# Conversions of the dense weights at other steps of the attention, a second buffer for their squares, and one choice of clusters that ends later

## Chip, cores and metric

One Trainium2 chip, one of its NeuronCores. The metric is the time of one execution on the device in microseconds, lower is better. TensorE (PE) multiplies, VectorE (DVE), ScalarE (ACT) and GpSimd (POOL) work on tiles, SyncE (SP) issues most transfers.

## The reference

The program is a chain of three layers. `q`, `k`, `v` have the shape (2, 8, 768, 64), with 16 clusters for each head.

```python
def _attn_ref(q, k, v, centroids):
    ...
    q_assign = np.argmax(np.einsum('bhsd,hcd->bhsc', q_n, c_n), axis=-1)
    k_assign = np.argmax(np.einsum('bhsd,hcd->bhsc', k_n, c_n), axis=-1)
    mask = q_assign[:, :, :, None] == k_assign[:, :, None, :]
    scores = scale * np.matmul(q, k.transpose(0, 1, 3, 2))
    scores = np.where(mask, scores, -1000000000.0)
    ...
    return np.matmul(attn, v).astype(np.float32)      # softmax over the allowed keys

def reference(**kwargs):
    attn_out = _attn_ref(**attn_kwargs)
    x = attn_out.transpose(0, 2, 1, 3).reshape(B * S, H * D)          # 1536 x 512
    x = _moe_ref(x=x, **moe_kwargs)    # each token to the best of 8 experts: relu(x @ w1[e]) @ w2[e], gated
    return _moe2_ref(x=x, **moe2_kwargs)   # h = x @ w_in; (h * sigmoid(1.702 h)) @ w_out, 2048 wide
```

The weights `w_in` and `w_out` of the last layer arrive as 64-bit floats.

## The kernel before

The kernel runs three stages one after another: attention (to about 265 us of the span), the experts, the dense layer. The change touches the attention alone.

**Units and steps.** Attention has 8 units u, each two heads of one batch entry. A unit has 12 steps, a step is one head and 128 queries against all 768 keys; there are 96 steps, and step i belongs to unit i // 12. The remainder r = i % 12 says where in its unit a step is. One turn i of the loop issues, in this order: the scores `sp` of step i + 1 (four matmuls on PE, L496 and L497) and their maximum `nm` (DVE, L499), pieces of the next units' preparation, conversions of dense weights, products with v, the transposes `pt` of step i - 1 (PE, L513) with their copies `pT` (first half on ACT, L518, second half on DVE, L520), and the exponential `P` of step i + 1 (ACT, L505). Each engine works through its own list in this order, so one instruction that waits holds up all behind it on that engine. The n-th `nm` in the trace is therefore a clock of the steps.

**Long and short steps.** In two places of a unit, at r = 2, 3 and at r = 8, 9, PE also multiplies with v: `po`, 24 matmuls (L548). Their result goes through `oa` on ACT (L554) and `pox` on PE (L567) to `xw` on DVE (L569).

**Preparation of a unit.** A table PLAN says at which step each of the ten pieces of a later unit is issued: transposes of q and k (`pqk`, PE, with `Fq`, `Fk` on ACT and `Hq`, `Lq`, `Hk`, `Lk` on POOL) and stacks (DMAs on SP to `Q`, `X`, `Z`), cluster scores (`pcl`, PE), and on DVE the choice of a cluster: `by_token` and `argmax_a` (L408 and L378 to L380), `argmax_b` (L387, a maximum `m2`), `chosen` (L392), `by_cluster` (L412); then `rows_of_ones` (ACT L416, 8 small DMAs `ohT` on SP). Piece 5 is issued late in r = 2, piece 6 (`argmax_b`) at the start of r = 3.

**Conversion of dense weights.** A quarter of the 64-bit weights (8 groups of 128 x 512 numbers out of 32) is turned into 32-bit numbers during the attention, and waits in DRAM (`wd`) for the dense layer. A group is loaded to `raw` (512 KB, SP), and four operations follow, named here after the code: `bits` (a square of the high word on ACT, L117, into the buffer `csq`, and a shift on DVE, L118), `top` (L121), `tail` (L124), `guard` (L127, which reads and overwrites `csq`). Behind `guard` stand a store of `csq` to `wd`, issued by POOL (L163), and the load of the next group. There is one `csq` buffer, so the square of the next group has to wait until that store has landed.

**What sets the order.** The dict `slots` says how many operations of this list step i issues:

```python
    slots = {12 * u + r: n for u in range(1, 5) for r, n in ((3, 1), (8, 1), (9, 2))}
    slots.update({11: 2, 68: 1, 69: 1, 75: 1, 80: 2, 81: 2, 86: 2, 87: 2, 92: 1, 93: 2})
    ...
            if i in (8, 11):
                load_early()
            for _ in range(slots.get(i, 0)):
                convert_early()
```

**Zeros.** `zrow` is 128 x 512 zeros; eight DMAs of 768 KB (`zero_rows`, L286) write them to `xd` at steps 14, 18, ... 42. Nobody reads `zrow` after that. From step 61 on, pieces of the routing of the first batch entry (`route(0)`) run between the attention's own operations, mostly on DVE and POOL.

Of the kernel before, what the change touches and what calls it, by code (L numbers as in the profile page):

```python
# [9 lines left out]
F32 = mybir.dt.float32  # L10
# [13 lines left out]
E = 8  # L24
# [21 lines left out]
def attention_moe_ffn(ctx: ExitStack, tc: tile.TileContext, q, k, v, centroids, w_gate, w_og, w1, w2, w_in, w_out, out):  # L46
# [3 lines left out]
    def f32(ap):  # L50
        return ap.bitcast(F32)
# [47 lines left out]
    def wide_load(pool, c, g):  # L99
        src = pair_of(w_in, w_out, c)[g // 2].bitcast(I32)  # L100
        t = pool.tile([128, 1024], I32, name="raw", tag="raw")
        if g < 2:
            nc.sync.dma_start(out=t.rearrange("p (k n) -> p k n", k=2), in_=src[:, 2 * g:2 * g + 2])
        else:
            nc.sync.dma_start(out=t, in_=src[:, g - 2])
        return t

    def wide_ops(pool, t, csq=2):

        r = t.rearrange("p (n w) -> p n w", w=2)  # L110
        l, h = r[:, :, 0], r[:, :, 1]
        hold = {}

        def bits():
            hold["t"] = pool.tile([128, 512], I32, name="ct", tag="ct", bufs=1)
            hold["s"] = pool.tile([128, 512], F32, name="csq", tag="csq", bufs=csq)
            nc.scalar.activation(hold["s"], f32(h), AF.Square)  # L117
            nc.vector.tensor_scalar(hold["t"], h, 3, 0x3FFFFFFF, op0=ALU.logical_shift_left, op1=ALU.bitwise_and)  # L118

        def top():  # L120
            nc.vector.scalar_tensor_tensor(hold["t"], h, -0x40000000, hold["t"], op0=ALU.bitwise_and, op1=ALU.bitwise_or)  # L121

        def tail():
            nc.vector.scalar_tensor_tensor(hold["t"], l, 29, hold["t"], op0=ALU.logical_shift_right, op1=ALU.bitwise_or)  # L124

        def guard():
            nc.vector.scalar_tensor_tensor(hold["s"], hold["s"], F64_TINY, f32(hold["t"]), op0=ALU.is_ge, op1=ALU.mult)  # L127
        return hold, [bits, top, tail, guard]
# [14 lines left out]
    cva = at.enter_context(tc.tile_pool(name="cva", reuse_waits="tile", bufs=2))  # L143
# [2 lines left out]
    ready = deque()  # L146
    convert = deque()

    def load_early():
        if early:  # L150
            c, g = early.pop(0)
            ready.append((c, g, wide_load(cva, c, g)))

    def convert_early():
        if not convert:
            if not ready:
                return
            c, g, t = ready.popleft()
            hold, ops = wide_ops(cva, t, 1)

            def last(f=ops[3]):
                f()
                nc.gpsimd.dma_start(out=wd[2 * c + g // 2][:, (g % 2) * 512:(g % 2) * 512 + 512], in_=hold["s"])  # L163
                load_early()
            convert.extend(ops[:3] + [last])
        convert.popleft()()
# [14 lines left out]
    fill = []  # L181
    scatters = []
    zrow = one.tile([128, DM], F32, name="zrow")

    def load_unit(u):
        b, pr = UNITS[u]
        d = st[u] = {}
        for nm, src in (("q", q), ("k", k), ("v", v)):
            t = ld.tile([128, 2, T, D], F32, name=f"ld_{nm}", tag=f"ld_{nm}", bufs=4 if nm == "v" else 2)
            nc.sync.dma_start(out=t, in_=src[b, 2 * pr:2 * pr + 2].rearrange("h (p t) d -> p h t d", t=T))  # L190
            d[nm] = t
# [16 lines left out]
    def setup_first():  # L208
        nc.vector.memset(idle, 0.0)
        keep_clock(7)  # L210
        nc.sync.dma_start(out=craw, in_=centroids.rearrange("h c d -> (h c) d"))
        load_unit(0)
        make_identity(nc, ident)
        nc.vector.tensor_copy(identb, ident)
        ii = one.tile([128, C], I32, name="ii")
        nc.gpsimd.iota(ii, [[-1, C]], base=C, channel_multiplier=0)
        nc.vector.tensor_copy(rev16, ii)
        nc.vector.memset(pen_scale[0:32], 1.0)
        nc.vector.memset(pen_scale[32:64], BIG)
        nc.vector.memset(pen_scale[64:80], BIG)  # L220
        nc.vector.memset(pen_bias[0:32], 0.0)
        nc.vector.memset(pen_bias[32:64], -BIG)
        nc.vector.memset(pen_bias[64:80], -BIG)

    def setup_centroids():
        nc.gpsimd.memset(nought, 0.0)

        csq = one.tile([128, D], F32, name="csq")
        cn = one.tile([128, 8], F32, name="cn")
        nc.vector.tensor_tensor(csq, craw, craw, op=ALU.mult)  # L230
        nc.vector.tensor_reduce(cn[:, 0:1], csq, op=ALU.add, axis=AX.X)
        nc.scalar.activation(cn[:, 1:2], cn[:, 0:1], AF.Sqrt)
        nc.scalar.activation(cn[:, 7:8], cn[:, 0:1], AF.Exp)
        nc.vector.tensor_scalar(cn[:, 2:3], cn[:, 1:2], 1e-30, None, op0=ALU.max)
        nc.vector.reciprocal(cn[:, 3:4], cn[:, 2:3])
        nc.vector.scalar_tensor_tensor(cn[:, 4:5], cn[:, 0:1], cn[:, 3:4], cn[:, 2:3], op0=ALU.mult, op1=ALU.add)
        nc.vector.tensor_scalar(cn[:, 5:6], cn[:, 4:5], 0.5, 1e-6, op0=ALU.mult, op1=ALU.add)
        nc.vector.reciprocal(cn[:, 6:7], cn[:, 5:6])
        cnorm = one.tile([128, 2, D], F32, name="cnorm")
        nc.vector.tensor_scalar(cnorm[:, 0], craw, cn[:, 6:7], None, op0=ALU.mult)  # L240
        nc.vector.tensor_copy(cnorm[:, 1], cnorm[:, 0])
        nc.vector.tensor_copy(cblk.rearrange("p h a c -> p (h a c)"), nought.to_broadcast([128, H * 4 * C]))
        return cnorm
# [236 lines left out]
    NS = len(steps)  # L480
# [279 lines left out]
            nc.vector.tensor_tensor(ci[:, b], t2, place[b], op=ALU.add)  # L760


    PLAN = ((0, 0, 0, 1, 3, 5, 6, 7, 8, 8), (-3, -2, 0, 1, 1, 2, 3, 8, 8, 9), (-2, -1, 0, 1, 1, 2, 3, 8, 8, 9))
    plan_at = {}
    for u in range(1, len(UNITS)):
        for n, r in enumerate(PLAN[min(u, 3) - 1]):
            plan_at.setdefault((12 * (u - 1) + r, n == 6, n == 5 and u > 1), []).append((u, n))
    pieces = {}

    def prepare(i, early=False, late=False):  # L770
# [3 lines left out]
            for f in pieces[u][n]:  # L774
                f()

    slots = {12 * u + r: n for u in range(1, 5) for r, n in ((3, 1), (8, 1), (9, 2))}
    slots.update({11: 2, 68: 1, 69: 1, 75: 1, 80: 2, 81: 2, 86: 2, 87: 2, 92: 1, 93: 2})

    with tc.manual_schedule():  # L780
        setup_first()
        first = prep_pieces(0)
        load_unit(1)
        cnorm = setup_centroids()
        for n, piece in enumerate(first):
            if n == 1:
                setup_blocks(cnorm)
            if n == 3:
                keep_clock(8)
            for f in piece:  # L790
                f()
        setup_rest()
        emit_scores(0)
        emit_exp(0)
        for i in range(NS + 2):
            nu, r = divmod(i + 3, 12)
            if i == 3 or r == 0 and nu + 2 < len(UNITS):
                load_unit(nu + 2)
            prepare(i, True)
            if i + 1 < NS:  # L800
                emit_scores(i + 1)
            tail = i >= NS - TAIL
            if (tail or i % 3 == 0) and ost:
                ost.popleft()()
            prepare(i)
            if i == 0:
                spots[:] = [(ps_m, "m")]
            if i >= 14 and i % 4 == 2 and len(fill) < E:
                zero_rows(len(fill))
            if i % (NS // 2) == NS // 2 - 4 and i < NS:  # L810
                sum_logits(i // (NS // 2))
            if i == NS // 2 + 13:
                routing.append(route(0))
            if i in (8, 11):
                load_early()
            for _ in range(slots.get(i, 0)):
                convert_early()
            for _ in range(2 if tail else 1):
                if av:
                    av.popleft()()  # L820
            prepare(i, False, True)
            if 0 <= i - 1 < NS:
                emit_pt(i - 1)
            n = i - (1 if tail else 2)
            if 0 <= n < NS and steps[n][2] % 3 == 2:
                queue_av(n)
            if i + 1 < NS:
                emit_exp(i + 1)
        advance(stop="weighed")
        while av:  # L830
            av.popleft()()
        while ost:
            ost.popleft()()
        advance()
        routing.append(route(2))
        advance()
        finish_routing()
        assert not (early or ready or convert)
        keep_clock_last(90)
# [315 lines left out]
    with tc.manual_schedule():  # L1155
# [23 lines left out]
        for g in range(G + 2):  # L1179
            e, c = divmod(g, 8)  # L1180
            nxt = wins.get(e + 1)
            r = c - (7 - nxt["nr"]) if nxt else 0
# [78 lines left out]
    with tc.manual_schedule():  # L1261
        gq = deque()
        for g in range(len(seq) + 2):
# [6 lines left out]
            if g >= 2:  # L1270

                for m in range(4) if g < len(seq) or g == len(seq) + 1 else ():
                    for g0, gh, gl in list(gq)[:1] if g < len(seq) else gq:
                        fh, tb, c, i = seq[g0]
# [47 lines left out]
```

## Time and profile before

| | |
|---|---|
| median of 3 runs | 744.75 us (744.46 to 746.16) |
| the profiled execution | 743.59 us, of which the span of its instructions 741.6 us |
| PE busy in the span | 709.2 us (96%) |
| DVE, ACT, POOL busy | 453.8, 390.2, 262.1 us |
| mean granted TensorE clock | 0.983 of full speed |

PE is called busy also while its pipelined matmuls are only being waited out, so 96% does not say that PE sets the time at each place. The rows below are from the same execution; their times count from the start of its span.

### The profile page before, as it was taken

The page shows a single profiled execution, that of the slowest core. Times are in us where ns is not written, and L with a number is a line of the kernel's source. Part 1 is how long each engine was busy: PE and PEld are TensorE (multiplying, and loading weights), DVE is VectorE, ACT ScalarE, POOL GpSimd, SP SyncE. Part 2 cuts the span into 40 slices and gives each one's busy share as a digit, 9 for nine tenths or more (in the row PEclk, how much of TensorE's full clock was granted, in tenths as well). Part 3 has the DMA queues.
Part 4 walks back from the last instruction along what each step waited for, and adds up shares of the span by engine and source line. Part 5 has one row for each costly group of instructions (what it writes and reads, how often), then busy time and mean ns, then how long its engine had stood idle before and what let it go on. Part 6 is the DMA issues. An engine that isn't in the chain of part 4 may idle for free.

```text
span 741.6 us, 12556 instructions
## 1 busy us (share of the span) xinstructions
PE 709.2 (96%) x4572; PEld 582.0 (78%) x4572; DVE 453.8 (61%) x855; ACT 390.2 (53%) x779; POOL 262.1 (35%) x216
## 2 busy tenths in 40 slices
PE   8999999999998887999999998999999999999996
PEld 5766786777766667999999897888888888888885
DVE  6969788789887772334554555687555656232322
ACT  7765675666755553455677776545434344222120
POOL 1230321303930033655778879122332212020202
PEclk9999999999999997999999999999999999999998
DMA  6779769555351037565576775134544211010101
GB/s 193 178 186 293 208 221 279 142 148 133 125 143 54 16 131 263 188 228 195 185 243 225 250 242 192 57 114 90 68 72 42 74 62 53 1 57 0 57 1 57
DMA packets 66689, 101.27 MB, mean 137 GB/s; under 512 B 9440, under 2 KB 44384, under 8 KB 66624
## 3 DMA queue, kind: packets, MB, share of 16 engines
q1 hardware_dynamic: 63680, 92.04, 43.4%
q0 software_dynamic: 2944, 8.40, 3.0%
q8 instruction: 37, 0.61, 0.4%
q14 instruction: 28, 0.23, 0.1%
HBM read 66.56 MB, written 14.69 MB: 110 GB/s over the span
## 4 chain that ended last, share of the span: by engine, by line
PE 59%; issue 18%; DVE 11%; ACT 6%; POOL 2%; DMA 2%; SPq 1%; POOLq 0%; ACTq 0%; DVEq 0%
PE pt L513 6%; PE po L548 6%; PE sp L496 4%; PE ph L1151 4%; PE ph L1150 4%; PE ph L1152 4%; PE sp L497 3%; PE py L1243 3%; PE py L1242 3%; PE py L1244 3%; ACT w L888 3%; PE py L974 2%; PE ph L974 2%; PE pox L567 2%; DVE nm L499 1%
## 5 line engine op out<-in xcount | busy, mean ns | idle before, releaser
L891 POOL TENSOR_TENSOR w<-raw,w 128x1024 fp32r<-128x1024 f32 x51 | 125.4, 2476 | 45.8 <-ACT w L888 30.5
L499 DVE TENSOR_REDUCE nm<-sp 128x1 f32<-128x768 f32 x96 | 91.6, 955 | 16.4 <-PE sp L497 14.5
L1227 DVE TENSOR_TENSOR sg<-ph,sg 128x512 f32<-128x512 f32 x48 | 33.2, 691 | 104.6 <-ACT sg L1226 104.2
L505 ACT ACTIVATE P<-sp,nm 128x768 f32<-128x768 f32 x96 | 87.5, 912 | 10.8 <-DVE nm L499 9.7
L513 PE MATMUL pt<-ident,P 128*128 128x128 f32 x576 | 84.4, 279 | 8.0 <-ACT pT L518 5.5
L513 PEld LDWEIGHTS pt<-ident,P 128*128 128x128 f32 x576 | 65.7, 142 | 32.5 <-issue 18.8
L1226 ACT ACTIVATE sg<-ph 128x512 f32<-128x512 f32 x48 | 28.7, 598 | 109.2 <-PE ph L1152 105.9
L1151 PE MATMUL ph<-ytl,w 128*128 128x512 f32 x192 | 76.1, 397 | 0.0
L1150 PE MATMUL ph<-yth,w 128*128 128x512 f32 x192 | 76.0, 396 | 0.0
L1152 PE MATMUL ph<-yth,w 128*128 128x512 f32 x192 | 75.5, 393 | 0.0
L924 POOL TENSOR_TENSOR w<-csq,w 128x512 fp32r<-128x512 f32 x24 | 32.8, 1365 | 120.5 <-ACT w L923 120.5
L1243 PE MATMUL py<-w,gh 128*128 128x512 f32 x192 | 75.3, 392 | 0.0
L496 PE MATMUL sp<-X,Q 128*128 128x384 f32 x192 | 74.0, 386 | 1.0 <-ACT P L505 0.9
L1242 PE MATMUL py<-w,gh 128*128 128x512 f32 x192 | 74.9, 390 | 0.0
L1244 PE MATMUL py<-w,gl 128*128 128x512 f32 x192 | 74.7, 389 | 0.0
L888 ACT CAST w<-raw 128x1024 fp32r<-128x1024 f32 x68 | 70.5, 1043 | 3.9 <-DMA raw<-in_moe_w_dram 3.9
L548 PE MATMUL po<-pT,ld_v 128*32 128x384 f32 x768 | 68.6, 490 | 0.0
L497 PE MATMUL sp<-Z,Q 80*128 80x384 f32 x192 | 65.9, 343 | 0.0
L518 ACT COPY pT<-pt 128x384 f32<-128x384 f32 x96 | 46.1, 480 | 37.5 <-PE pt L513 37.3
L974 PE MATMUL py<-ht,w 128*128 128x480 f32 (+5 forms) x192 | 60.8, 368 | 4.3 <-DVE ht L998 2.9
L520 DVE COPY pT<-pt 128x384 f32<-128x384 f32 x96 | 52.8, 550 | 14.1 <-PE pt L513 14.0
L974 PE MATMUL ph<-t,w 128*128 128x480 f32 (+5 forms) x192 | 60.3, 367 | 0.0
(253 smaller groups left out, 1504.9 us busy)
## 6 DMA issues: line engine op xcount, KB each, us to landing
raw<-in_moe_w_dram SPq DMA_DIRECT2D x64, 512.0 KB, 4.1
raw<-in_moe_w_in_dram SPq DMA_DIRECT2D x16, 512.0 KB, 5.2
raw<-in_moe_w_out_dram SPq DMA_DIRECT2D x16, 512.0 KB, 3.3
xd<-zrow SPq DMA_DIRECT2D x8, 768.0 KB, 6.5
Q<-Hq SPq DMA_DIRECT2D x28, 192.0 KB, 3.8
ld_q<-in_q_dram SPq DMA_DIRECT2D x8, 384.0 KB, 4.7
ld_k<-in_k_dram SPq DMA_DIRECT2D x8, 384.0 KB, 6.1
ld_v<-in_v_dram SPq DMA_DIRECT2D x8, 384.0 KB, 7.7
```

The lines of the kernel that those rows point to most:

```text
L496: nc.tensor.matmul(sp[:, n, :384], d["Q1"][:, h, cs], d["X"][:, h, ks], start=True, stop=False)
L499: nc.vector.tensor_reduce(nm, sp[:, :, :384], op=ALU.max, axis=AX.XY, negate=True)
L513: nc.tensor.transpose(pt[:, r * 128:(r + 1) * 128], L["P"][:, n, r * 128:(r + 1) * 128], ident)
L548: nc.tensor.matmul(po[32 * g:32 * g + 32, :384], v_[:, hh, tile_t(kt), 32 * a:32 * a + 32], pts[n][:, kt, :], start=kt < (2 if alone else ...
L891: (eng or nc.gpsimd).tensor_tensor(lo, r, f32(hi), op=ALU.subtract)
L974: nc.tensor.matmul(ps[:, :2 * n], w_hi, t, start=first, stop=False)
L1150: nc.tensor.matmul(ph, wa(key, 0, k, i), yth[:, k, cs], start=(k == 0), stop=False)
L1151: nc.tensor.matmul(ph, wa(key, 0, k, i), ytl[:, k, cs], start=False, stop=False)
L1152: nc.tensor.matmul(ph, wa(key, 1, k, i), yth[:, k, cs], start=False, stop=(k == 3))
L1242: nc.tensor.matmul(po[m], gh[:, ms], wb(key, 0, i), start=first, stop=False)
L1243: nc.tensor.matmul(po[m], gh[:, ms], wb(key, 1, i), start=False, stop=False)
L1244: nc.tensor.matmul(po[m], gl[:, ms], wb(key, 0, i), start=False, stop=last)
```

## The change

The same operations are done, on the same data. Four things move. (1) The first two loads of dense weights go from steps 8 and 11 to steps 15 and 18, and the table of conversions is shifted: nothing at 11, 15 and 20, three at 21, the pattern of r = 3, 8, 9 in units 2 to 5 instead of 1 to 4, and a new distribution from 75 on. (2) The square's buffer is one tile that is kept, and from step 48 on `zrow` is a second one; groups 3, 5 and 7 use it. (3) `argmax_b` of unit 2 goes from the start of step 15 to step 20, ahead of `chosen` and `by_cluster`. (4) With that, each operation lands in another kind of step, as this table shows (b = bits, t = top, l = tail, g = guard):

| step | 11 | 15 | 20 | 21 | 27 | 32 | 33 | ... | 63 | 68 | 69 | 75 | 80 | 81 | 86 | 87 | 92 | 93 |
|---|---|---|---|---|---|---|---|---|---|---|---|---|---|---|---|---|---|---|
| before | bt | l | g | bt | l | g | bt | | | l | g | b | tl | gb | tl | gb | t | lg |
| after | | | | btl | g | b | tl | | g | b | tl | g | b | tl | gbt | lg | bt | lg |

Steps 39, 44, 45 and 51, 56, 57 go as 27, 32, 33 do.

```diff
-    def wide_ops(pool, t, csq=2):
+    def wide_ops(pool, t, square=None):
...
-            hold["s"] = pool.tile([128, 512], F32, name="csq", tag="csq", bufs=csq)
+            hold["s"] = pool.tile([128, 512], F32, name="csq", tag="csq") if square is None else square
...
+    spare_squares = []
...
-            hold, ops = wide_ops(cva, t, 1)
+            if not spare_squares:
+                spare_squares.append(cva.tile([128, 512], F32, name="csq", tag="csq", bufs=1))
+            hold, ops = wide_ops(cva, t, spare_squares[(4 * c + g) % len(spare_squares)])
...
-    PLAN = ((0, 0, 0, 1, 3, 5, 6, 7, 8, 8), (-3, -2, 0, 1, 1, 2, 3, 8, 8, 9), (-2, -1, 0, 1, 1, 2, 3, 8, 8, 9))
+    PLAN = ((0, 0, 0, 1, 3, 5, 6, 7, 8, 8), (-3, -2, 0, 1, 1, 2, 8, 8, 8, 9), (-2, -1, 0, 1, 1, 2, 3, 8, 8, 9))
...
-            plan_at.setdefault((12 * (u - 1) + r, n == 6, n == 5 and u > 1), []).append((u, n))
+            plan_at.setdefault((12 * (u - 1) + r, n == 6 and u != 2, n == 5 and u > 1), []).append((u, n))
...
-    slots = {12 * u + r: n for u in range(1, 5) for r, n in ((3, 1), (8, 1), (9, 2))}
-    slots.update({11: 2, 68: 1, 69: 1, 75: 1, 80: 2, 81: 2, 86: 2, 87: 2, 92: 1, 93: 2})
+    slots = {12 * u + r: n for u in range(2, 6) for r, n in ((3, 1), (8, 1), (9, 2))}
+    slots.update({21: 3, 27: 1, 75: 1, 80: 1, 81: 2, 86: 3, 87: 2, 92: 2, 93: 2})
...
+            if i == NS // 2:
+                assert len(fill) == E
+                spare_squares.append(zrow)
-            if i in (8, 11):
+            if i in (15, 18):
                 load_early()
```

The list of PE is the same row for row. Three places on the other engines follow; line numbers behind the change are 4 to 7 higher.

ACT at steps 80 to 82 before: `P` is the exponential, `ohT` the one-hot rows of unit 7, the square into `csq` stands between `ohT` and `oa`.

```order
L518 COPY pT<-pt 128x3x128
L505 ACTIVATE P,sm<-sp,nm 128x768
L416 ACTIVATE ohT<-oT,oh_bias,oh_scale 128x384
L117 ACTIVATE csq<-raw 128x512
L554 COPY oa<-po 128x384
L518 COPY pT<-pt 128x3x128
```

ACT at the same steps of the change: the square stands one `pT` and one `P` earlier, and it writes `zrow`.

```order
L117 ACTIVATE zrow<-raw 128x512
L522 COPY pT<-pt 128x3x128
L509 ACTIVATE P,sm<-sp,nm 128x768
L420 ACTIVATE ohT<-oT,oh_bias,oh_scale 128x384
L558 COPY oa<-po 128x384
L522 COPY pT<-pt 128x3x128
```

So no square is left between `ohT` and `oa`; the same move was made at steps 33, 45 and 57, with `csq` or `zrow` as its buffer.

DVE at step 15 before, where unit 2's choice stands between the scores of unit 1:

```order
L380 TENSOR_TENSOR eq<-eq,rev_60 128x384
L520 COPY pT<-pt 128x3x128
L387 TENSOR_REDUCE m_911<-eq 128x24
L499 TENSOR_REDUCE nm<-sp 128x1
L569 TENSOR_TENSOR xw_107<-pox,rs 128x3x80
L124 SCALAR_TENSOR_TENSOR ct<-raw,ct 128x512
L520 COPY pT<-pt 128x3x128
L499 TENSOR_REDUCE nm<-sp 128x1
```

DVE at the same step of the change:

```order
L384 TENSOR_TENSOR eq<-eq,rev_60 128x384
L524 COPY pT<-pt 128x3x128
L503 TENSOR_REDUCE nm<-sp 128x1
L573 TENSOR_TENSOR xw_107<-pox,rs 128x3x80
L524 COPY pT<-pt 128x3x128
L503 TENSOR_REDUCE nm<-sp 128x1
```

The maximum L387 and the `tail` L124 are gone from here; the maximum stands at step 20 now, where `guard` stood.

SP behind the stacks of unit 2 in the change (`xd<-zrow` are the zero fills of steps 14 and 18, the first two loads of dense weights stand behind one each, then come the loads of unit 4 and the one-hot rows of unit 2):

```order
L290 DMA xd<-zrow 128x3x512
L103 DMA raw<-in_moe_w_in_dram 128x2x512
L290 DMA xd<-zrow 128x3x512
L103 DMA raw<-in_moe_w_in_dram 128x2x512
L194 DMA ld_q<-in_q_dram 128x2x384
L194 DMA ld_k<-in_k_dram 128x2x384
L194 DMA ld_v<-in_v_dram 128x2x384
L426 DMA Z<-ohT 16x384 x2
```

Before, both loads stood further up, one ahead of the loads of unit 3 and one ahead of the stacks of k, and the place here held two fills and the third load.

## Rows read from the trace of the kernel before

**Rows 1.** Timeline of ACT: squares at steps 11, 21 and 81, with their wait.

```profile
47.44 0.67 ACT L117 ACTIVATE csq<-raw 128x512 f32<-128x512 f32 x1 [3.68 <-DMA raw<-in_moe_w_in_dram]
...
74.06 0.66 ACT L117 ACTIVATE csq<-raw 128x512 f32<-128x512 f32 x1 [2.34 <-DVE rs L558]
...
227.20 0.66 ACT L117 ACTIVATE csq<-raw 128x512 f32<-128x512 f32 x1 [3.58 <-issue]
```

**Rows 2.** Timeline of PE: what it waited for behind two of them.

```profile
48.53 0.90 PE L567 MATMUL pox<-wl,oa 128*128 128x80 f32 x6 [1.61 <-ACT oa L554]
...
228.66 0.71 PE L513 MATMUL pt<-ident,P 128*128 128x128 f32 x3 [1.93 <-ACT pT L518]
```

**Rows 3.** Timeline of DVE: maxima nm, steps 21, 25, 33, 36, 37, 45, 49.

```profile
67.26 0.96 DVE L499 TENSOR_REDUCE nm<-sp 128x1 f32<-128x768 f32 x1
...
79.19 0.96 DVE L499 TENSOR_REDUCE nm<-sp 128x1 f32<-128x768 f32 x1 [0.23 <-PE sp L497]
...
98.19 0.96 DVE L499 TENSOR_REDUCE nm<-sp 128x1 f32<-128x768 f32 x1
...
107.08 0.96 DVE L499 TENSOR_REDUCE nm<-sp 128x1 f32<-128x768 f32 x1 [0.23 <-PE sp L497]
...
108.78 0.96 DVE L499 TENSOR_REDUCE nm<-sp 128x1 f32<-128x768 f32 x1 [0.23 <-PE sp L497]
...
127.75 0.96 DVE L499 TENSOR_REDUCE nm<-sp 128x1 f32<-128x768 f32 x1
...
139.27 0.96 DVE L499 TENSOR_REDUCE nm<-sp 128x1 f32<-128x768 f32 x1 [0.23 <-PE sp L497]
```

**Rows 4.** Timeline of DVE: maxima nm, steps 83, 84, 85, then 89, 90, 91.

```profile
226.34 0.96 DVE L499 TENSOR_REDUCE nm<-sp 128x1 f32<-128x768 f32 x1 [0.21 <-PE sp L497]
...
231.30 0.96 DVE L499 TENSOR_REDUCE nm<-sp 128x1 f32<-128x768 f32 x1 [1.34 <-PE sp L497]
...
233.28 0.96 DVE L499 TENSOR_REDUCE nm<-sp 128x1 f32<-128x768 f32 x1 [0.23 <-ACT P L505]
...
244.02 0.96 DVE L499 TENSOR_REDUCE nm<-sp 128x1 f32<-128x768 f32 x1 [0.21 <-PE sp L497]
...
248.12 0.96 DVE L499 TENSOR_REDUCE nm<-sp 128x1 f32<-128x768 f32 x1 [0.84 <-PE sp L497]
...
249.50 0.96 DVE L499 TENSOR_REDUCE nm<-sp 128x1 f32<-128x768 f32 x1
```

**Rows 5.** Windows, behind the stall of step 81: columns end with clock, DMA share, GB/s.

```profile
228.60:231.00 2.40, 2.16 (x8) 1.67 (x9) 0.56 (x1) 2.16 (x6) 0.00 (x0) 0.56 0.48 145
```

**Rows 6.** Timeline of DVE at step 15.

```profile
58.34 0.54 DVE L387 TENSOR_REDUCE m<-eq 128x24 f32<-128x384 f32 x1
58.80 0.95 DVE L499 TENSOR_REDUCE nm<-sp 128x1 f32<-128x768 f32 x1
```

**Rows 7.** Sources L118 and L127: min/median/max ns of bits and guard.

```profile
L118 DVE TENSOR_SCALAR ct<-raw x32: 410/419/1537, 47.4 to 625.0; 128x512 int32<-128x512 int32 x32
...
L127 DVE SCALAR_TENSOR_TENSOR csq<-csq,ct x32: 648/684/693, 69.2 to 630.5; 128x512 f32<-128x512 f32 x32
```

**Rows 8.** Timeline of unit 2: idle time of ACT at r = 8, DVE at r = 9.

```profile
100.67 0.48 ACT L518 COPY pT<-pt 128x384 f32<-128x384 f32 x1 [1.90 <-PE pt L513]
...
104.59 0.56 DVE L520 COPY pT<-pt 128x384 f32<-128x384 f32 x1 [0.48 <-PE pt L513]
```

**Rows 9.** Timeline of PE at step 64.

```profile
181.79 0.55 PE L513 MATMUL pt<-ident,P 128*128 128x128 f32 x3 [0.49 <-DVE pT L520]
```

**Rows 10.** Tile csq, then tile raw to 290 us: transfers from issue to landing.

```profile
DMA to landing us min/median/max: 2.3/2.4/4.3
...
DMA to landing us min/median/max: 3.5/5.7/9.0
```

**Rows 11.** Timeline: fills on SP, and bits of the second group on DVE (step 21).

```profile
58.91 2.10 SPq L286 DMA_DIRECT2D xd<-zrow  x2
...
71.73 0.42 DVE L118 TENSOR_SCALAR ct<-raw 128x512 int32<-128x512 int32 x1
```

## Prediction

> **What bounds the kernel now.** I read the page first: PE is called busy for 96% of the span, and the attention is a third of it. Then I read PE's own waits from 20 us on, and then, backwards in the timelines of ACT and DVE, what stood ahead of each. All of PE's waits of over 1.1 us from there to the last maximum lead to an instruction that the change moves. The maxima `nm` serve as the clock of the steps: what a stall costs is how much later the next maxima come than they do in the same place of a unit without that stall. This is safer than to add up idle times, because a wait on ACT can be hidden by PE's products.
>
> Two things hold the squares. At step 11 ACT sits 3.68 us until the first group of dense weights has landed [rows 1]; `oa` is queued behind the square, `pox` on PE waits for `oa`, and PE is idle for 1.61 us [rows 2]. At step 21 and at step 81 the square waits although its data is there: what came last by the profile had long been done or was not seen ("rs", "issue"), and the square starts at 74.06 and 227.20 [rows 1]. What it waits for is the store of `csq`, since `guard` of the group before stands one step (21, 33, 45, 57) or no step at all (81, 87) ahead of it, and such a store takes 2.3 to 4.3 us to land [rows 10]. Steps 45 and 87 stall in the same way; 33 and 57 get away with it.
>
> **The change part by part.** All times below are of the profiled execution, 743.59 us, of which 741.6 are the span; it lies 1.16 us (0.16%) under the median of the runs shown, which I add at the end.
>
> *First loads at steps 15 and 18, no conversion at 11.* Nothing on ACT stands between the exponential and `oa` at step 11 any more. PE has run through all that it could and then sat 1.61 us [rows 2]; that is the gain. Below, it is nothing if the same wait comes again at step 21, which is the first rival. The work that goes from here (a square, 0.66 us, and two operations of DVE) was hidden in the wait.
>
> *Step 15.* `argmax_b` of unit 2 stands between the choice and `nm` there, and DVE has no idle time ahead of either; its successor starts 0.46 us after it [rows 6]. ACT and PE wait for this `nm`, so 0.46 us is the gain. `tail` leaves the same step behind that `nm`; as long as `guard`, at 0.68 us [rows 7], it could add that much, but PE is still busy with the next scores at that point. I take nothing for it and keep 0.68 as the upper end. At step 20 the maximum takes the place of `guard`, is shorter (0.54 against 0.68), and the wait of DVE for PE behind it covered the longer one.
>
> *Squares at r = 8, guards at r = 3.* From `guard` to the next square there are now five steps instead of none or one. At r = 8 ACT waits 1.90 us for PE ahead of its `pT` [rows 8], so a square of 0.66 us is covered there; if that cover were gone it would cost 0.66 each. What the old waits cost, from the maxima:
> - Step 21: from nm of step 21 to that of step 25 it takes 79.19 - 67.26 = 11.93 us; a unit later, with the same operations and a store that landed in time, 108.78 - 98.19 = 10.59 [rows 3]. Gain 1.34.
> - Step 45: 139.27 - 127.75 = 11.52 against 10.59 [rows 3]. Gain 0.93. In this stretch lies also a sum of logits on DVE; I take it as hidden by PE's products, and if it is not, this gain is nothing.
> - Step 81: from step 83 to 84 it takes 231.30 - 226.34 = 4.96 us [rows 4]. A step without `po` takes 108.78 - 107.08 = 1.70 with transposes of a next unit in it [rows 3], and 249.50 - 248.12 = 1.38 without [rows 4]. I take 1.70 and keep 1.38 for the range: 3.26. Then the clock: behind this stall of 1.93 us [rows 2] the granted clock was 0.56 from 228.6 to 231.0, so mostly at the lower of its levels (1.2 GHz of 2.4) [rows 5], and the step to 233.28 took 1.98 instead of 1.38 [rows 4]: another 0.60, which goes with the stall. Together 3.86.
> - Step 87: 248.12 - 244.02 = 4.10 [rows 4], less 1.70: 2.40.
>
> *The second buffer.* `zrow` was read last by the zero fills, issued by step 42; its first square stands at step 56, and 12 steps take 127.75 - 98.19 = 29.6 us [rows 3], against 9.0 us for the longest load here [rows 10]. It costs nothing, and it is what lets steps 86 and 92 hold a square with the last store still under way. With `csq` alone, five steps apart would do until step 80.
>
> *What is added.* At step 63 a `guard` comes into a stretch where DVE is full (choice of unit 6 and routing together) and PE waits for DVE's copies, 0.49 us at 181.79 [rows 9]: 0.68 us in full. At step 75 `guard` takes the place of `bits`: 0.68 - 0.42 = 0.26 [rows 7], also in full, as at r = 3 the choice leaves DVE no room. At r = 9 `top` and `tail` take the place of `bits` and `top`, 0.26 more, ahead of a copy for which DVE waits 0.48 us [rows 8]: covered, 0. At step 21 there are three, 0.68 more than now against 0.48 of cover; 0.20 late, which the 0.23 us wait of the next maxima takes up [rows 3]: 0, and 0.20 for the range. Steps 86, 87, 92 and 93 lie in the last unit, which prepares nothing, and their long steps hold three operations: 0. The stores on POOL go with their guards; what is queued behind them is a transform of two steps later or a routing row that waits for DVE anyway: 0.
>
> *Sum.* Gains 1.61 + 0.46 + 1.34 + 0.93 + 3.86 + 2.40 = 10.60 us; costs 0.68 + 0.26 = 0.94. Net 9.66. 743.59 - 9.66 = 733.9; against the median, 744.75 - 9.66 = 735.1 us. All of it lies ahead of the experts, who start from rows that attention scatters and can't start earlier, so it passes to the end.
>
> *A rule that speaks against it.* The trace has stores landing 2.3 to 4.3 us after issue [rows 10], and the guards now stand in steps where DVE runs without a gap [rows 6]. The Trainium skill ("SBUF — State Buffer", section "SBUF: two separate sides") says that a transfer issued from GpSimd can wait as long as VectorE holds the port that the two share, since its descriptors can't be written; on its account the moved stores could land later than now. No run here shows one that did. What late stores would cost is the fourth rival.
>
> **The rivals.**
> *The wait of step 11 comes again at step 21.* The first fill is issued at 58.91, and two take 2.10 us [rows 11], so the first load is issued by about 61, behind 768 KB of zeros, and `bits` of step 21 starts at 71.73 [rows 11]. That is 10.7 us in the old clock; step 11's 1.61 and step 15's 0.46 move both ends. The longest load here took 9.0 us [rows 10]. Against it stands also that two loads of 512 KB are gone ahead of this place. If it is late by 3 us, what steps 11 and 21 give (1.61 + 1.34) is gone: 738.0. Chance 7%.
> *The long stalls go only in part.* At steps 81 and 87 something else is next: the one-hot rows of unit 7 are copied to their stacks by eight DMAs on SP behind step 81's `ohT`, and the first scores of unit 7 need them; if those land late, or PE's clock drops there all the same, half of 3.86 + 2.40 stays: 738.2. For it: only the ACT wait is visible now, what lies under it is not. Against it: between steps 33 and 37 the same rows did not hold PE. Chance 10%.
> *Nothing changes.* Something else would have to hold the experts' start. The profile has nothing there that does not come from the attention. 744.7. Chance 2%.
> *Stores that take twice as long as the worst.* From the maximum behind r = 3 to that behind r = 8 there are 67.26 - 58.80 = 8.5 us [rows 3, 6]. A store over that would stall four units by 1.34 each, 5.4 us: 740.5. Chance 2%.
> *Slower than before.* The first load, or the transfers in which it stands, is so late that step 21 pays more than all the rest gives: it would have to land over 9.66 us past 71.73, so more than 20 us after its issue at 61 [rows 11]. From this point on it decides; at 22 us it would give 746. Nothing in the trace comes near. Chance 2%.
>
> **How the numbers follow.** My sum has the remaining 77%. Its own range goes down by 0.68 (`tail`) and twice 0.32 (1.38 for 1.70) and 0.26 (step 75 hidden), to 733.5, and up by 0.20 (step 21), 0.66 (a square not hidden in one place) and 0.93 (the stall at 45 not from the square), to 736.9. The first two rivals end at 738; I set the range from 732.5 to 738.5, which leaves out the last three rivals and a little at each end. Runs of this kernel spread over 0.2%, 1.5 us, and that is the bound between faster and same: faster 0.96, same 0.02, slower 0.02.
>
> **What would show it.** Right: PE has no wait of over 1.1 us from 44 us to the last maximum; squares on ACT start within 0.1 us of the instruction ahead or in a wait for PE; the clock stays at 1.00 in the attention's last 40 us; the maxima around steps 21, 45, 83 and 89 come as in the undisturbed units; the last maximum of the attention comes some 9.7 us earlier; from there on all is as before. Wrong: ACT or DVE waits for `raw` at step 21; `sp` at step 84 waits for a DMA `ohT`; the maxima behind step 63 lose more than 1 us; or the experts take longer by what the attention gave.

## The result, and the profile after

The changed kernel takes 733.55 us in the median of 6 runs (730.86 to 735.02), the kernel before 744.61 us (6 runs, 743.79 to 746.55): 11.06 us less; the ratio, formed over all the runs, is 0.984 (95% interval 0.9816 to 0.9864). The forecast was 735.1 us, 9.66 less, with a range from 732.5 to 738.5. The profiled execution took 733.66 us, 731.9 of them span, at a mean TensorE clock of 0.983 as before.

PE's waits from 20 us to behind the last maximum (engine, line, what it waited for: total, times, longest):

```profile
PE pt L517 <- ACT pT L522: 1.5, 2, 1.0
PE pt L517 <- DVE pT L524: 1.5, 6, 0.4
PE sp L500 <- ACT P L509: 0.4, 1, 0.4
PE sp L501 <- DMA Q<-ohT: 0.3, 1, 0.3
```

Nothing over 1.0 us is left, and `pox` waits for `oa` no more [rows 2]. The squares at steps 21, 80 and 86 on ACT's timeline stand without the waits that they had [rows 1]:

```profile
69.69 0.71 ACT L117 ACTIVATE csq<-raw 128x512 f32<-128x512 f32 x1
...
216.19 0.67 ACT L117 ACTIVATE zrow<-raw 128x512 f32<-128x512 f32 x1
...
230.08 0.70 ACT L117 ACTIVATE csq<-raw 128x512 f32<-128x512 f32 x1
```

A part of these waits stands in another view: by source line, the semaphore waits of ACT's own queue ahead of the squares (min/median/max ns). First the kernel before, from 20 to 262 us, then the changed one from 20 to 252:

```profile
L117 ACTq EVENT_SEMAPHORE  x6: 17/1979/5298, 70.1 to 239.3; - x6
```

```profile
L117 ACTq EVENT_SEMAPHORE  x8: 17/17/38, 95.1 to 243.1; - x8
```

Three of the six waits of before, at steps 21, 81 and 87, are 3.9 to 5.3 us long; the other three, at 33, 45 and 57, read 17 ns (1979 is the middle between 17 and the shortest of the long ones). After the change none is over 0.04. But the 17 ns don't mean that those squares were free. At step 45 ACT sat idle for 1.94 us, and the store of `csq` that was issued at 131.72 took 2.3 us to land. POOL and ACT of the kernel before:

```profile
131.72 0.56 POOL L163 DMA_DIRECT2D wd<-csq  x1 [18.02 <-DMA ld_v<-in_v_dram]
...
134.14 0.67 ACT L117 ACTIVATE csq<-raw 128x512 f32<-128x512 f32 x1 [1.94 <-DVE rs L558]
```

All six squares, those with 17 ns too, started less than 0.1 us behind the landing of the store ahead of them. That, with run 1 below, is what says that the store held them. The maxima `nm` around steps 21 to 25, then 83 to 85 and 89 to 91, as in [rows 3, 4]:

```profile
65.34 0.96 DVE L503 TENSOR_REDUCE nm<-sp 128x1 f32<-128x768 f32 x1 [0.20 <-PE sp L501]
...
72.52 0.96 DVE L503 TENSOR_REDUCE nm<-sp 128x1 f32<-128x768 f32 x1
74.77 0.96 DVE L503 TENSOR_REDUCE nm<-sp 128x1 f32<-128x768 f32 x1 [0.78 <-PE sp L501]
76.47 0.96 DVE L503 TENSOR_REDUCE nm<-sp 128x1 f32<-128x768 f32 x1 [0.23 <-PE sp L501]
...
222.89 0.96 DVE L503 TENSOR_REDUCE nm<-sp 128x1 f32<-128x768 f32 x1 [0.22 <-PE sp L501]
224.29 0.96 DVE L503 TENSOR_REDUCE nm<-sp 128x1 f32<-128x768 f32 x1
226.02 0.96 DVE L503 TENSOR_REDUCE nm<-sp 128x1 f32<-128x768 f32 x1 [0.31 <-PE sp L501]
...
236.71 0.96 DVE L503 TENSOR_REDUCE nm<-sp 128x1 f32<-128x768 f32 x1 [0.16 <-PE sp L501]
238.11 0.96 DVE L503 TENSOR_REDUCE nm<-sp 128x1 f32<-128x768 f32 x1
239.89 0.96 DVE L503 TENSOR_REDUCE nm<-sp 128x1 f32<-128x768 f32 x1 [0.35 <-PE sp L501]
```

Step 83 to 84 takes 1.40 us where it took 4.96, and 89 to 90 takes 1.40 where it took 4.10; the next step takes 1.73 for 1.98 and 1.78 for 1.37. The clock stays at full speed over the last 41 us of the attention (window; the number behind the counts of POOL is the clock, then DMA share and GB/s):

```profile
210.00:251.00 41.00, 40.91 (x340) 29.93 (x339) 36.91 (x60) 28.46 (x60) 1.65 (x3) 1.00 0.26 77
```

From the first maximum to the last, the attention took 242.92 us before, 232.23 in this execution and 232.56 in a second one of the same kernel, profiled later (run 7 below). The table gives what each place gained (a minus is a loss), from the same intervals of maxima in the three traces (step 87: from 88 to 91).

| place | forecast | first | second |
|---|---|---|---|
| step 11, first load and square | 1.61 | 1.89 | 1.89 |
| step 15, `argmax_b` and `tail` | 0.46 | 1.06 | 1.07 |
| step 21, square | 1.34 | 0.80 | 1.35 |
| step 45, square | 0.93 | 0.94 | 0.87 |
| step 63, `guard` added | -0.68 | -0.60 | -0.60 |
| step 75, `guard` for `bits` | -0.26 | 0.52 | -0.33 |
| step 81, square, with the clock | 3.86 | 3.81 | 3.82 |
| step 87, square | 2.40 | 2.35 | 2.36 |
| all others | 0 | -0.08 | -0.07 |
| sum | 9.66 | 10.69 | 10.36 |

What lies outside is not the change's: the first maximum came 1.02 us later than before in the first execution (18.35 for 17.33), and over all the executions profiled here it comes between 17.2 and 18.8 whichever kernel it is; the time from the last maximum to the end of the span is 481.3 us before and after. So the experts took nothing back.

### The profile page after: what moved, and what is told of

The parts are those of the page before. It is cut to its first block, busy times and chain, and to the rows that moved or that the text cites. A ratio compares the mean times of both kernels' runs of the same rounds, so it can differ in the third digit from the quotient of the medians.

```text
span 731.9 us, 12553 instructions
## 1 busy us (share of the span) xinstructions
PE 706.3 (96%) x4571; PEld 581.1 (79%) x4572; DVE 454.1 (62%) x855; ACT 391.7 (54%) x779; POOL 261.2 (36%) x216
## 4 chain that ended last, share of the span: by engine, by line
PE 60%; issue 17%; DVE 10%; ACT 5%; DMA 3%; POOL 3%; SPq 1%; POOLq 0%; ACTq 0%; DVEq 0%
PE po L552 7%; PE pt L517 6%; PE sp L500 4%; PE ph L1158 4%; PE ph L1157 4%; PE ph L1159 4%; PE sp L501 3%; PE py L1250 3%; PE py L1249 3%; PE py L1251 3%; ACT w L895 3%; PE py L981 2%; PE ph L981 2%; PE pox L571 2%; PE ph L977 1%
```

## The experiments

Every run stands beside the kernel before on the same chip; its medians there were 745.08, 746.09 and 744.83 us in the three groups (runs 1 to 4, 5 to 8, 9 and 10). My theory throughout: the squares wait for the store out of their only buffer, the square of step 11 for its load, and DVE has no room at r = 3.

**1. Two buffers, everything else as before.**

```diff
-    idle = one.tile([128, 512], BF16, name="idle")
+    idle = zrow.bitcast(BF16)[:, 0:512]        # zeros too; makes room
-            hold, ops = wide_ops(cva, t, 1)
+            hold, ops = wide_ops(cva, t, 2)
```

> The kernel before, with two csq buffers in turn and nothing else (the same steps, loads and choice; to make room, the tile of zeros for the first matmuls is a view of zrow). Theory: the squares of steps 21, 45, 81 and 87 wait for the store of the one csq buffer. Then these four stalls are gone although the squares stand where they stood: gains of 0.8 to 1.34, 0.93, 3.86 and 2.40, in all 8.0 to 8.5 us, so about 736 us; the stall of step 11 stays, since it waits for the load. Rival: it is their place between ohT and oa, or their data, that holds them, and only the new steps help: the stalls stay, 744 us.

Measured: 736.88 us (4 runs), ratio 0.9875 (0.983 to 0.9919). The maxima gained 1.34 at step 21, 0.93 at 45, 3.04 + 0.61 at 81 and 2.70 - 0.33 at 87, with the squares in their old places: the store was the cause, not the place. From first to last maximum the gain is 6.4 us; the median gained 8.2, so that it met the expectation partly by what lies outside the attention. Step 11 stayed and cost 1.94 us more in this execution: 0.34 at the first maximum behind the wait, which was longer, and 1.60 in the step behind that, where the clock was low. ACT, then PE there, and a window behind it:

```profile
49.01 0.67 ACT L117 ACTIVATE csq<-raw 128x512 f32<-128x512 f32 x1 [4.01 <-DMA raw<-in_moe_w_in_dram]
```

```profile
50.10 1.57 PE L567 MATMUL pox<-wl,oa 128*128 128x80 f32 x6 [1.93 <-ACT oa L554]
```

```profile
51.00:53.00 2.00, 2.00 (x12) 2.00 (x12) 1.11 (x2) 0.82 (x4) 0.10 (x1) 0.50 1.06 323
```

PE sat 1.93 us instead of 1.61, and from 51 to 53 us its granted clock was 0.50, the lower level of 1.2 GHz. The six `pox` took 1.57 us.

**2. The change with one buffer only.**

```diff
-                spare_squares.append(zrow)
```

> The change with its new steps, but csq alone as buffer (zrow never becomes the second). Theory: five steps between guard and square are enough for the store, so nothing changes up to step 85; at step 86 the square stands behind the guard of the same step and waits for its store, as it did at step 87 before: 2.3 to 2.7 us more than the change. Rival: the stores of other steps come too late as well (descriptors written late, as they now fall where DVE is full): stalls also at 32, 44, 56, 68 or 80, over 4 us more.

Measured: 733.43 us (2 runs), ratio 0.9841 (0.9788 to 0.9894), no loss that shows against the change. The expectation for step 86 failed. The wait is there, up to 4.6 us on ACT's queue, in that queue's row by source line and on ACT's timeline:

```profile
L117 ACTq EVENT_SEMAPHORE  x7: 17/17/4592, 94.5 to 243.5; - x7
```

```profile
234.07 0.71 ACT L117 ACTIVATE csq<-raw 128x512 f32<-128x512 f32 x1 [3.65 <-DVE pT L524]
```

But of the maxima behind it one came 0.17 us later, the next another 0.24, and the third had 0.22 of that back: ahead of `pT` at r = 2 ACT would have waited for PE's 24 products anyway. At r = 9 the same wait had held up `oa`. The second buffer is thus worth 0.2 us once the steps are moved, and 8.3 us where they are not (run 1): either of the two edits alone takes away nearly all that the wait for the store cost.

**3. The choice of unit 2 back at step 15.**

```diff
-    PLAN = (..., (-3, -2, 0, 1, 1, 2, 8, 8, 8, 9), ...
+    PLAN = (..., (-3, -2, 0, 1, 1, 2, 3, 8, 8, 9), ...
-            plan_at.setdefault((12 * (u - 1) + r, n == 6 and u != 2, ...
+            plan_at.setdefault((12 * (u - 1) + r, n == 6, ...
```

> The change, with unit 2's argmax_b back at the start of step 15. In the change the maximum of step 16 came 0.45 us earlier against its neighbours, that of step 17 another 0.61. Theory: the 0.45 is argmax_b's and the 0.61 is the tail's that left step 15; so this run loses 0.45 at step 16, keeps the 0.61, and gives at most 0.1 back at step 20. Rival: both are argmax_b's, and this run loses 1.06.

Measured: 733.07 us (one run). The maximum of step 16 came 0.45 us later, as forecast, and the 0.61 us behind it stayed gained. So that part is not `argmax_b`'s; run 9 asks whose it is.

**4. The second load later.**

```diff
-            if i in (15, 18):
+            if i in (15, 24):
```

> The change, with the second load of dense weights at step 24 instead of 18. In the change the step to the maximum of step 24 took 2.25 us, 0.54 more than in an undisturbed unit, and PE waited 0.29 us for a DMA of one-hot rows. Theory: those rows queue behind the transfers of step 18 (a fill and this load); with the load gone from there the step takes 1.70 to 1.75 and 0.5 us is won. Rival: the rows land in their usual time and the wait has another cause: 2.25 stays.

Measured: 733.06 us (one run). Step 23 to 24 took 1.70 us instead of 2.25, but it took 1.71 and 1.70 in runs 2 and 3 as well, with the load in its place at 18. The run does not tell the two apart; what differs is the execution (run 7).

**5. Guards one step earlier.**

```diff
+    for i in (27, 39, 51, 75):
+        slots[i - 1] = slots.pop(i)
```

> The change, with the guards of steps 27, 39, 51 and 75 (r = 3) issued one step earlier, at r = 2, where DVE waits 1.72 us for the cluster scores pcl ahead of the choice. Theory: at r = 3 DVE runs without a gap and every operation there is paid in full, at r = 2 it is covered. Then the interval between the maxima behind these steps falls by about 0.5 us in each of the four units (by about 0.3 at 75, where only the longer guard counts against before), and the median is about 2 us under that of the change in the same job (ratio to it 0.997). Rival: the guard is covered at r = 3 as well, or DVE's copies at r = 2 come later by as much; then the median stays within 0.3 us of the change.

Measured: 731.72 us (6 runs) beside 733.81 for the change (run 7): 2.09 less, as expected in sum but not in its parts: steps 27, 39 and 51 gave 0.24 us each where 0.5 was expected, and step 75 gave 1.22 for 0.3. DVE around the maximum of step 76 in the change (run 7), then here:

```profile
204.58 0.91 DVE L383 TENSOR_TENSOR eq<-sc,m 128x384 f32<-128x384 f32 x1
205.53 1.25 DVE L384 TENSOR_TENSOR eq<-eq,rev 128x384 f32<-128x384 f32 x1
...
207.62 0.94 DVE L503 TENSOR_REDUCE nm<-sp 128x1 f32<-128x768 f32 x1
208.49 0.67 DVE L127 SCALAR_TENSOR_TENSOR csq<-csq,ct 128x512 f32<-128x512 f32 x1
...
209.82 0.95 DVE L503 TENSOR_REDUCE nm<-sp 128x1 f32<-128x768 f32 x1
```

```profile
200.28 0.98 DVE L127 SCALAR_TENSOR_TENSOR csq<-csq,ct 128x512 f32<-128x512 f32 x1
202.08 0.58 DVE L412 STREAM_TRANSPOSE sc<-pcl 128x384 f32<-128x384 f32 x1 [0.82 <-PE pcl L409]
...
203.29 0.79 DVE L383 TENSOR_TENSOR eq<-sc,m 128x384 f32<-128x384 f32 x1
204.11 0.74 DVE L384 TENSOR_TENSOR eq<-eq,rev 128x384 f32<-128x384 f32 x1
...
205.70 0.94 DVE L503 TENSOR_REDUCE nm<-sp 128x1 f32<-128x768 f32 x1
...
207.30 0.95 DVE L503 TENSOR_REDUCE nm<-sp 128x1 f32<-128x768 f32 x1
```

The guard now lies in the wait for `pcl`, and 0.60 us of 1.22 is the step from 76 to 77 without it (1.60 for 2.20). The other 0.62 lies ahead of it: the choice's two-input operations took 1.53 us together, not 2.16. That is their meeting with POOL, below; the change's own two executions differ there by as much, so this run does not show that the edit gave it.

**6. Two buffers, and nothing at r = 3 or at step 63.** As run 1 makes room, with the change's loads and this table:

```diff
+    slots = {21: 2, 26: 2, 32: 1, 33: 2, 38: 2, 45: 2, 50: 2, 56: 1, 57: 2, 69: 2, 74: 2,
+             80: 1, 81: 2, 86: 3, 87: 2, 92: 2, 93: 2}
```

> The change with two csq buffers from the start (the operand of the first matmuls, zeros as well, becomes a view of zrow to make room), and a table without any operation at r = 3 and none at step 63: 21 two, then r = 2 two (lg), r = 8 one and r = 9 two by turns. Theory: what is left of the conversions' price after the change is what stands at r = 3 and at step 63 (guards, 0.5 to 0.6 us each); two buffers keep the squares free of the stores wherever they stand. Then about 2.6 us under the change, some 0.6 under the kernel with guards at r = 2. Rival: two operations at r = 2 are more than the 1.72 us there cover next to the copies, or the squares at r = 9 hold oa up; then no gain over the kernel with guards at r = 2, or a loss.

Measured: 729.94 us (6 runs), ratio to the kernel before 0.979 (0.9761 to 0.9818), 3.9 under the change. From first to last maximum it gained 1.81 us on run 7. Its places: 0.24 at each of 27, 39 and 51, 0.59 at 63, 0.23 at 69, 0.83 at 75, with a loss of 0.52 at step 24 to a late `ohT` and 0.2 around steps 83 to 86. Without the late `ohT` it is 2.3, somewhat under the 2.6 expected; the median says more than the maxima do.

**7. The change again.**

> The changed kernel as it is, beside the others of this job. Theory: the 0.54 us that step 21 gave less than forecast (a wait of PE for the rows ohT) and the 0.78 us that step 75 gave more were of that one execution; in this profile the interval from the maximum of step 23 to that of step 24 is 1.7 us and that over step 75 6.9 us, as in two of the experiments. Rival: they belong to the kernel, and come again as 2.25 and 6.07 us. The ratio to the kernel before is again 0.984.

Measured: 733.81 us (6 runs), ratio 0.9827 (0.9797 to 0.9858). Step 23 to 24 took 1.70 and the step to 76 took 6.92: the first execution's 2.25 and 6.07 were its own; 6.9 stands in runs 2, 3, 4 and 9 as well. In tile `ohT` between 60 and 80 us, from issue to landing, the first execution, run 6 (both with the late step) and this one read:

```profile
DMA to landing us min/median/max: 1.9/2.3/3.7
```

```profile
DMA to landing us min/median/max: 1.9/1.9/3.6
```

```profile
DMA to landing us min/median/max: 1.9/1.9/2.6
```

Runs 2 and 5, without a late step, have 2.8 and 2.4 as their slowest.

**8. The kernel before, with its first load at step 5.**

```diff
-            if i in (8, 11):
+            if i in (5, 11):
```

> The kernel before, with its first load of dense weights at step 5 instead of 8, so that on SP it stands ahead of the one-hot rows of unit 1 and not behind them; all conversions stay where they are. Theory: step 11 was late for nothing but the landing of that load, so its wait of 3.68 us on ACT and 1.61 us on PE goes, the maximum of step 13 comes 1.6 to 2.2 us earlier, the other stalls stay, and the median is about 1.6 us under the kernel before. Rival: the square and the shift are themselves in the way of oa at step 11; then at least 0.66 us of it stays. Second rival: the load now delays the one-hot rows on SP, and the first scores of unit 1 wait for them.

Measured: 742.58 us (12 runs), ratio 0.9963 (0.9937 to 0.9988). Both the theory and the second rival came true. The square of step 11 started at 43.60 without a wait, `oa` waited for nothing but PE, and maxima 13 and 14 gained 1.87 us. But maximum 12 lost 1.15, since PE waited 0.92 us at 43.69 for `ohT`, whose transfers were issued at the same times as before and landed in up to 4.7 us instead of 2.0. The load took away what it gave but for 0.7 us. The median's 3.5 us are twice the 1.6 expected. Of the 2.6 us between first and last maximum, the stalls at steps 21 and 81, shorter in this execution, gave another 1.0 and 1.3, and the one at 45, longer, took 0.5. Why they came out so stays open, and the rest of the median's gain no trace shows.

**9. The work of `tail` put back at step 15.**

```diff
+            if i == 15:
+                same = cva.tile([128, 512], I32, name="ct", tag="ct", bufs=1)
+                zi = zrow.bitcast(I32)
+                nc.vector.scalar_tensor_tensor(same, zi, 29, zi, op0=ALU.logical_shift_right, op1=ALU.bitwise_or)
```

> The change with one operation of DVE added at step 15, where tail stood before: the same form and size as tail, on the zeros of zrow, its result used by nobody. Theory: the second part of step 15's gain, 0.61 us behind the maximum of step 16, came from tail's leaving, so it is paid in full there: the interval from the maximum of step 16 to that of step 17 goes back from 1.64 to about 2.25 us, and the interval ahead of it stays at 5.42. Rival: the 0.61 us came from something else that moved (the first load, or the squares); then the interval stays at 1.64. The median shows little of it, 0.6 us of 733.

Measured: 733.72 us (4 runs). DVE at that step:

```profile
57.88 0.95 DVE L503 TENSOR_REDUCE nm<-sp 128x1 f32<-128x768 f32 x1
...
59.06 0.68 DVE L826 SCALAR_TENSOR_TENSOR ct<-zrow 128x512 int32<-128x512 int32 x1
...
60.12 0.95 DVE L503 TENSOR_REDUCE nm<-sp 128x1 f32<-128x768 f32 x1
```

From 57.88 to 60.12 is 2.24 us, against 1.64 without it and 2.25 in the kernel before. An operation of `tail`'s form and size takes the whole 0.61 back.

**10. Run 6 once more.**

> The kernel with two buffers and no operation at r = 3 or at step 63, once more. In the job before it came out 3.9 us under the change, where the maxima of its profiled execution gave 1.8 us and another 0.5 for a wait for ohT. Theory: the maxima tell what the table is worth, about 2.3 us, and the rest is the spread of the parts ahead of and behind the attention; then the start of the first maximum and the time from the last one to the end are as in the other kernels (about 18 and 481 us), and the median is near 731.4. Rival: the table or the view of zrow shortens the start or the experts too, and the profile shows them short again (17.2 and 478.9 us).

Measured: 730.02 us (6 runs), ratio 0.9799 (0.9776 to 0.9823). From first to last maximum it takes 230.24 us, 2.32 less than the change, as expected; the start is back at 18.72, and behind the last maximum lie 479.4 us (728.4 of span less 248.96). But the median came out 1.4 us below the 731.4 expected, as in run 6. Those 479.4 are 1.5 to 1.9 less than the change's 480.95 and 481.32, yet runs 2 and 9, with the change's own tables but for their edit, have 479.4 and 479.9 too. Whether this kernel really shortens what comes behind the attention stays open. It is the fastest of all: 3.9 us under the change in the one group (run 7), and in the other 3.7 under run 9, which is the change with one operation added.

## Why the forecast was right, point by point

**The stalls.** Steps 21, 45, 81 and 87 measured 8.40 us in the second execution against 8.53 forecast, and run 1 shows that the store alone was behind them. Steps of the unit next door without the stall were the right measure: no term is off by over 0.06. At step 81 that is partly luck. The sum was 3.26 for the step to 84 and 0.60 for the clock in the next; the change gave 3.56 and 0.26, since a step without the stall takes 1.40 and then 1.72 there, not 1.70 and 1.38. With everything in its old place (run 1) the two are 1.92 and 1.37, so 3.04 and 0.61: the clock's 0.60 was right for that order and went with the stall.

**The sum.** The attention gave 0.7 to 1.0 us more than the 9.66 forecast, most of it at steps 15 and 11, below. That the profiled span fell by 9.7 us (741.6 to 731.9), so nearly by the forecast, is luck: the first maximum came 1.02 later in this execution.

**Step 11** was forecast at 1.61 us, PE's wait [rows 2], and gave 1.89. The wait was the right mechanism, its row too small a size. PE's rows there, before and after:

```profile
46.58 0.33 PE L497 MATMUL sp<-Z,Q 80*128 80x384 f32 x1
48.53 0.67 PE L567 MATMUL pox<-wl,oa 128*128 128x80 f32 x4 [1.61 <-ACT oa L554]
```

```profile
47.58 0.34 PE L501 MATMUL sp<-Z,Q 80*128 80x384 f32 x1
47.76 0.79 PE L571 MATMUL pox<-wl,oa 128*128 128x80 f32 x6
```

Without a wait `pox` starts 0.18 us behind the start of the last `sp`, ahead of its modelled end; with it 1.95 us. That is 1.77, and the six `pox` then took 0.90 [rows 2] instead of 0.79: 1.88. The idle time shown ahead of `pox` leaves out the overlap that the wait has broken.

**Step 15** is where a step of the reasoning failed. `argmax_b` gave its 0.46 us, but I took nothing for `tail`, because "PE is still busy with the next scores at that point", and it gave 0.61 more (run 9). The trace of before had rows against it. PE, then DVE there:

```profile
59.50 0.34 PE L497 MATMUL sp<-Z,Q 80*128 80x384 f32 x1
...
61.20 0.55 PE L513 MATMUL pt<-ident,P 128*128 128x128 f32 x3 [1.03 <-ACT pT L518]
```

```profile
59.98 0.68 DVE L124 SCALAR_TENSOR_TENSOR ct<-raw,ct 128x512 int32<-128x512 int32 x1
...
61.05 0.95 DVE L499 TENSOR_REDUCE nm<-sp 128x1 f32<-128x768 f32 x1
```

The scores that the `nm` at 61.05 reads were done at 59.84, ahead of `tail`'s start: DVE, not PE, was late here, and it had no gap in which `tail` could have been free. PE's wait at 61.20 was 1.03 us, under the threshold of 1.1 that I had set. It is 0.41 us with `argmax_b` alone at step 15 (run 3), 0.57 with the work of `tail` alone (run 9), and gone without both.

**What is added.** `guard` at 63 cost 0.60 of 0.68. At 75 the change cost 0.33 in the second execution, against 0.26, and gave 0.52 in the first, where DVE happened to meet POOL otherwise than before (last section). Runs 5 and 6 show that the guards at r = 3, which I had priced at nothing in units 2 to 4 since such an operation stood there before, cost 0.24 us each; the difference to before is nothing all the same, as forecast. The other steps cost nothing, as forecast.

**The second buffer.** "It is what lets steps 86 and 92 hold a square" was too strong: without it 0.2 us are lost (run 2).

**The rivals.** The first load did not hold step 21: its square shows no wait, and nobody waited for `raw`. Of the second rival's two causes the clock did not drop, and the rows `ohT` did hold `sp`, but at step 24 and in two executions only. The mechanism of the fourth was there without its price. Transfers out of `csq`, then out of `zrow`, from issue to landing:

```profile
DMA to landing us min/median/max: 2.3/5.9/7.1
```

```profile
DMA to landing us min/median/max: 2.3/3.9/8.5
```

Before they took 2.3 to 4.3 [rows 10]; those issued at r = 3 of units 2 to 4 now took 7.1, 6.3 and 5.9, and with the guards one step earlier (run 5) none out of `csq` took over 4.8. The Trainium skill ("SBUF — State Buffer", section "SBUF: two separate sides") has GpSimd's transfers wait while VectorE holds the port that they share, and a slower landing agrees with it. But traffic would do as well, and the rows lean to it. The DMA engines were busy for 0.95 to 1.00 of the time while these three stores were under way (88.4 to 95.6, 118.0 to 124.3 and 147.5 to 153.5 us), the first two of them beside fills of 768 KB (the 8.5 us are such a fill), and for 0.87 to 0.94 in run 5. Beside the three stores of before that landed in 2.3 to 2.4 us at steps 32, 44 and 56 it was 0.28 to 0.33, and at step 44 DVE was busy for 2.33 of the 2.40 us. No run changes the one without the other, so the cause is not shown. Five steps of cover took it up either way.

## What to carry over

When one buffer ties a cheap operation to a slow store, compare when the operation starts with when the store lands: here each start followed a landing by less than 0.1 us. The semaphore waits of that engine's queue by source line showed only three of the six, and the engine's idle time names whatever came last. Then give the store time (other steps) or a second buffer; one of the two is nearly enough, and which one is decided by what else the moved work meets. Price a stall by start-to-start intervals in a place without it, and read all waits along a full engine's chain, the short ones too: the term that I missed lay in a wait just under the threshold that I had set.

## What I had not expected of the hardware

**DVE operations with two inputs stretch beside POOL.** At step 75 of run 7 `eq` (L384) took 1.25 us, where 0.56 is usual, while POOL's `Lk` ran:

```profile
204.58 0.50 POOL L334 CAST Hk<-Fk 128x384 fp32r<-128x384 f32 x1
205.16 1.20 POOL L335 TENSOR_TENSOR Lk<-Fk,Hk 128x384 fp32r<-128x384 f32 x1
```

L383 began with POOL's cast at 204.58 and ended 0.41 us behind the cast's end; L384 began at 205.53 and ended 0.42 behind the end of `Lk` at 206.36: as if each had waited for POOL's operation and done most of its own 0.56 us behind it. The first execution shows the other order. DVE, then POOL:

```profile
204.63 0.56 DVE L383 TENSOR_TENSOR eq<-sc,m 128x384 f32<-128x384 f32 x1
205.22 0.74 DVE L384 TENSOR_TENSOR eq<-eq,rev 128x384 f32<-128x384 f32 x1
```

```profile
204.66 0.89 POOL L334 CAST Hk<-Fk 128x384 fp32r<-128x384 f32 x1
```

Here L383 was 0.03 us ahead, kept its 0.56, and the cast took 0.89 instead of 0.50. L383 and L384 took 1.30 us together here and 2.16 there: that is the 0.85 us by which the step to 76 differs between two executions of one kernel. A maximum with one input beside them (L382) took 0.55 in both. The Trainium skill (the same page and section) describes an exclusive lock between a GpSimd operation that reads SBUF and a VectorE operation with two inputs there, which goes to whichever starts first; these rows agree with it.

**The clock fell behind one wait of PE at step 11 and not behind another.** Before, PE waited 1.61 us there and the granted clock stayed at 1.00 from 48.5 to 56 us; in run 1 it waited 1.93 us and the clock was 0.50 for the 2 us from 51. Behind the 1.93 us of step 81 it had fallen as well [rows 2, 5]. No run here shows what decides it.
